# Row 0 by one queue, and a shorter run of idle matmuls ahead of the first product

## The chip, the cores and the metric

The kernel runs on one core of a Trainium2 chip. The metric is the device time of one execution in microseconds (us). TensorE (PE in the profile) multiplies, with its weight loads shown as PEld. VectorE (DVE), ScalarE (ACT) and GpSimd (POOL) work beside it on SBUF and PSUM, and transfers between DRAM and SBUF are issued by SyncE (SP), ACT and POOL and carried by 16 DMA engines.

## The reference, cut to what matters

```python
xn = layernorm(x)                                  # x: 2048 x 640, over the 640
h  = layernorm(xn)
a, b = xn @ dft_hid_re.T, xn @ dft_hid_im.T
fnet  = dft_seq_re @ a - dft_seq_im @ b            # 2048 x 640
mixer = (w2.T @ gelu(w1.T @ h + b1) + b2)          # over the 2048 tokens
out = x + fnet + mixer                             # float32
```

Here the kernel multiplies by the sequence DFT first (the transposed matrix against the normalized rows, both parts real and imaginary) and by the hidden DFT afterwards. The sums are the same.

## The kernel before

All matrix products are made in three passes of float32r operands: every operand is split into a high and a low part by `high` (an ACT copy that rounds) and `low` (a DVE subtraction), and `three` adds high x high, high x low and low x high into one PSUM bank. The `x` rows are cut into 16 blocks of 128 ("row k"), the sequence matrices into pieces of 128 x 512. The sequence product, the hidden product, the up product with the gelu and the down product follow each other. Each step of that list has three parts, `steps[i]`: the high part of a piece, its low part, and the products. `turn_of` runs them with the loads and sums that belong to a step.

The change lies at the very beginning, where the order is written out by hand in `START`, one word for each piece of work:

- The first line gives the loads in SP's order. `x0` is row 0, `b0` the first piece of the sequence matrix (`load`, line 507), `b1` the second, then `x1`, `b2` and so on. `x0` calls `row(0)` (line 545), which loads the first 320 columns of row 0 only. The other 320 columns were already asked of ACT's queue on line 137. That issue waits for a memset of POOL on line 136 that writes 128 of the same columns.
- Row 0 is normalized while it arrives. `M0` takes its moments (line 231, one DVE instruction for each half), `A0` puts them together (line 234), `R0` is the reciprocal root on ACT (line 240, tile `near`).
- `T0-0` and `T0-1` make the high part of piece 0: ACT its first 256 columns (line 151, called from line 196), DVE the other 256 (line 207). Behind ACT's half stands a small idle matmul on that half (line 197).
- `D0-0`, `D0-1`, `D0-3` make blocks of the normalized high part of row 0 on DVE (line 398), `H0-2-4` one on ACT (line 292). Each block is a weight of the first products.
- `P0-0` are the five first products (line 521): weights from row 0, 512 columns of piece 0 moving. Then `P0-1`, `P1-0`, `P1-1`, `P0-2`, `P1-2` follow, 24 products of row 0 altogether, and then `P2` and the rest, which need row 1 (`x1`, moments at line 231 too, high parts by `H1-0-2` and `H1-2-5`).

Ahead of all that stand the idle matmuls of line 148 on a constant: they write a PSUM bank that is used later from the start, and they wait for nothing. There are `WARM` of them, nine of 512 columns and six of 64.

Eight semaphores are handed round among the DMAs of SP and ACT, so SP's ninth and later DMAs each wait for the landing of the one eight places before.

Of the kernel before, what the change touches and what calls it, by code (L numbers as in the profile page):

```python
# [14 lines left out]
P = 128  # L15
S = 2048
D = 640
# [8 lines left out]
CH = 512  # L26
NC = S // CH
H2 = D // 2
EPS = 1e-5
AHEAD = 2  # L30
LOADS = 4
WARM = 15

BLOCK = 10
APART = 2
# [42 lines left out]
def fnet_plus_mixer(  # L78
# [30 lines left out]
    nc = tc.nc  # L109
# [19 lines left out]
    x_rows = [x[t * P : (t + 1) * P, :] for t in range(NS)]  # L129
# [3 lines left out]
        keep.tile([P, 7, D], F32, name="x0", tag="slab4"), keep.tile([P, 1, D], F32, name="x1", tag="slab5"),  # L133
    ]
    x_in = [x_slab[k // 7][:, k % 7, :] for k in range(8)]
    nc.gpsimd.memset(x_in[0][:, H2 : H2 + P], 0.0)
    nc.scalar.dma_start(x_in[0][:, H2:], x_rows[0][:, H2:])
    part_up = [dram.tile([P, 2, D], F32, name=f"up{r}") for r in range(NF2)]
    y_part = [[dram.tile([P, ND, CH], F32, name=f"y{m}{c}") for c in range(NC)] for m in range(2)]

# [3 lines left out]
    psum = [acc.tile([P, CH], F32, name=f"psum{i}") for i in range(8)]  # L144
    idle = nc.const_aps.tensor(1.0, [P, CH], dtype=BF16)
    for i in range(WARM):
        n = CH if i < WARM - 6 else P // 2
        nc.tensor.matmul(psum[7][:, :n], idle[:, :P], idle[:, :n], start=True, stop=True)  # L148

    def high(hi, src):  # L150
# [32 lines left out]
    def cut_piece(source, n, tail=False, stacked=False):  # L183

        held = {}

        def of_tail():
            hi, src = (t.rearrange("p (q c) -> p q c", c=P) for t in (held["piece"][:, 0, :n], source()))  # L190
            return hi[:, :, :TAIL], hi[:, :, P - TAIL :], src[:, :, :TAIL]

        def top(part=None):
            if part:
                hi = held["piece"][:, 0, : n // 2]
                high(hi, source()[:, : n // 2])
                nc.tensor.matmul(psum[7][:, : P // 2], hi[:, :P], hi[:, : P // 2], start=True, stop=True)  # L197
                return
            cut_turn[0] = (cut_turn[0] + 1) % (AHEAD + 1)
            held["piece"] = keep.tile([P, 2, D], R32, name="piece", tag=f"cut{cut_turn[0]}")  # L200
            if tail:
                hi, _, src = of_tail()
                high(hi, src)
            elif part is None:
                high(held["piece"][:, 0, :n], source())
            else:
                nc.vector.tensor_copy(held["piece"][:, 0, n // 2 : n], source()[:, n // 2 :])

        def bottom():
            if tail:  # L210
                hi, lo, src = of_tail()
                low(lo, src, hi)
                return held["piece"][:, 0, :n], None
            hi, lo = (held["piece"][:, i, :n] for i in range(2))
            if stacked:
                last = slice(n - P, n)
                low(hi[TAIL:, last], source()[TAIL:, last], hi[TAIL:, last])
            whole = n - P if stacked else n
            low(lo[:, :whole], source()[:, :whole], hi[:, :whole])
            return hi, lo  # L220

        return top, bottom
# [13 lines left out]
    def root(var, q=None):  # L236

        if q is None:
            q = small.tile([P, NS], F32, name="q")[:, : var.shape[-1]]
        nc.scalar.activation(q, var, AF.Abs_reciprocal_sqrt, bias=eps)  # L240
        return var, q
# [25 lines left out]
    def offset(to, ks):  # L267
        nc.vector.scalar_tensor_tensor(to[:, 1, ks], mv[:, ks, 0], -1.0, to[:, 0, ks], op0=ALU.mult, op1=ALU.mult)
# [134 lines left out]
    def channels(k, j):  # L403

        a = fixed[0][k % 4]
        i = (0, 0, 6, 6)[j] if k < 4 and j < 4 else (1, 1, 2, 2)[j] if j < 4 else None
        if i is None:
            return fifth(a, 0, k // 4), fifth(a, 1, k // 4)
        at = at_slot[i] + j % 2 * P
        return a[:, 0, at : at + P], a[:, 1, at : at + P]  # L410
# [76 lines left out]
    def c_tile():  # L487

        i = c_turn[0] = (c_turn[0] + 1) % 6
        return c_place[i // 3][:, i % 3, :]  # L490

    def store_y(add, m, c, j, t):
        if not add:
            nc.gpsimd.dma_start(y_part[m][c][:, j, :], t)
        else:
            nc.gpsimd.dma_start(y_part[m][c][:, j, :], t, accum_op=ALU.add)  # L496

    def first_columns():


        raw = pieces[1].rearrange("p a q c -> p (a q) c")
        banks = {}
        vq = {}

        def load(i):
            m, k = FIRST[i][:2]
            nc.sync.dma_start(raw[:, FIRST_AT[i], :], dft_seq[m * NC, k])

        def products(w, m, k, j0, j1, passes=(0, 1, 2)):


            late_begin = 4
            js = (range(3), range(3, 5)) if (m, k) == (1, late_begin) else (range(j0, j1),)
            if (m, k) == (0, 0):
                js = ((0, 1, 4, 2, 3),)
            for n, j in ((n, j) for part in js for n in passes for j in part):
                rows, cols = ((0, 0), (0, 1), (1, 0))[n]
                begin, end = (late_begin, 1) if m == 1 and j >= 3 else (0, 5)
                if n == 0 and k == begin:
                    banks[m, j] = psum[(5 * m + j) % 8]  # L520
                nc.tensor.matmul(  # L521
                    banks[m, j], channels(k, j)[rows], w[cols], start=n == 0 and k == begin,
                    stop=n == 2 and k == end, skip_group_check=True,
                )

        def read(m, js):
            for j in js:
                c = c_tile()
                nc.scalar.activation(c, banks[m, j], AF.Copy)
                store_y(False, m, 0, j, c)  # L530

        for i, (m, k, j0, j1) in enumerate(FIRST):
            steps.append(
                cut_piece(lambda i=i: raw[:, FIRST_AT[i], :], CH)
                + (lambda w, *passes, at=(m, k, j0, j1): products(w, *at, *passes),)
            )
        reads[6].append(lambda: read(0, range(ND)))

        extras[11].append(lambda: read(1, range(2)))
        extras[12].append(lambda: read(1, range(2, 4)))  # L540
        extras[13].append(lambda: read(1, range(4, ND)))

        def row(k):
            if k == 0:
                nc.sync.dma_start(x_in[0][:, :H2], x_rows[0][:, :H2])
            else:
                nc.sync.dma_start(x_in[k], x_rows[k])

        def begin_loads(i):
            for f in loads.pop(i):  # L550
                f()

        def top(i, *part):
            steps[i][0](*part)

        def bottom(i):
            ready[i] = steps[i][1]()

        def run(i, *passes):
            steps[i][2](ready[i], passes or (0, 1, 2))  # L560
            if not passes or 2 in passes:
                del ready[i]

        def rooted(k, to=None, by=1):
            ks = slice(k, (to or k) + 1, by)
            vq[k] = root(mv[:, ks, 1], near[:, 0, ks])

        def inverted(k, to=None, by=1):
            inverse(norm[:, 0, slice(k, (to or k) + 1, by)], *vq[k])

        def factored(k, to=None, by=1):
            inverted(k, to, by)
            offset(norm, slice(k, (to or k) + 1, by))

        def whole_row(k, by_vector=False):
            if not by_vector and k not in LAST_ROWS:
                return normalize(k, x_in[k], norm)

            nc.vector.tensor_scalar(
                x_in[k], x_in[k], mv[:, k, 0:1], norm[:, 0, k : k + 1], op0=ALU.subtract, op1=ALU.mult  # L580
            )

        return {
            "x": row, "b": load, "q": begin_loads, "T": top, "B": bottom, "P": run,
            "M": lambda k, *halves: statistics(k, x_in[k], *halves), "A": aggregate,
            "R": rooted, "F": factored, "O": lambda k: offset(near, slice(k, k + 1)), "E": half_beside, "V": factors_beside, "v": lambda k: factors_beside(k, False), "n": lambda k: whole_row(k, True), "e": lambda k: half_beside(k, nc.vector), "w": lambda k: factors_beside(k, False, nc.vector),
            "D": first_hi,
            "m": lambda k: nc.vector.tensor_scalar(less, mv[:, k, 0:1], -1.0, None, op0=ALU.mult),
            "c": lambda k: nc.scalar.activation(near[:, 1, k : k + 1], less, AF.Copy, scale=near[:, 0, k : k + 1]),
            "H": lambda k, *ends: first_rows(k, 0, *ends), "N": whole_row,  # L590
            "L": lambda k, *ends: first_rows(k, 1, *ends),
            "W": lambda k: nc.scalar.activation(one, eps, AF.Abs_reciprocal_sqrt),
        }
# [718 lines left out]
```

## Time and profile before

| | us |
|---|---|
| median of 3 runs | 866.1 |
| lowest, highest | 866.06, 866.36 |
| the profiled execution | 866.67 |
| its span, first to last instruction | 864.8 |
| PE busy | 860.9 |
| PEld busy | 790.1 |
| DVE busy | 695.0 |
| ACT busy | 524.0 |
| POOL busy | 159.9 |

The profiled execution took 1.9 us more than its span, which lies around the first and last instruction. All stretches below are counted from the start of the span. A matmul's shown duration holds the time in which its results drain, and matmuls overlap, so the distance between two starts tells how fast they are carried out. The row of the granted clock shows full speed in every slice.

### The profile page before, as it was taken

Reading aid. Unit: us, or ns where it says so; the run is one execution under the profiler, and the core shown is the slowest. Engines: PE = TensorE matmul, PEld = TensorE weight load, DVE = VectorE, ACT = ScalarE, POOL = GpSimd, SP = SyncE. Lnnn points to the kernel's source line nnn. Section 1 sums busy time; section 2 is a strip of 40 time slices with the busy share of each in tenths; the row PEclk is TensorE's granted clock in tenths of the full one; section 3 lists DMA queues with packets and bytes.
Section 4 is the critical chain, followed back from the end, with each engine's and each line's share of the span. In section 5 each row is a group of like instructions: output and inputs, shape, how many; then the busy total and the mean of one; then the engine's idle time right before and its main releaser. Section 6 shows DMA issues by size and latency. Waiting matters only on the chain.

```text
span 864.8 us, 13911 instructions
## 1 busy us (share of the span) xinstructions
PE 860.9 (100%) x4900; PEld 790.1 (91%) x4900; DVE 695.0 (80%) x1176; ACT 524.0 (61%) x970; POOL 159.9 (18%) x216
## 2 busy tenths in 40 slices
PE   9999999999999999999999999999999999999998
PEld 7888888888888888889999999999999999999998
DVE  7898868758767888677877788888679978987887
ACT  5765576763555555547565556676667866555654
POOL 2222131210020211122110101111322221101211
PEclk9999999999999999999999999999999999999999
DMA  9949586695382746869576666665688798766776
GB/s 339 366 102 271 183 254 226 161 292 152 98 188 31 193 105 131 217 108 200 125 167 160 156 142 195 189 175 160 143 185 182 167 235 224 182 142 126 158 168 149
DMA packets 90293, 154.44 MB, mean 179 GB/s; under 512 B 9008, under 2 KB 37424, under 8 KB 89968
## 3 DMA queue, kind: packets, MB, share of 16 engines
q0 software_dynamic: 25008, 57.52, 35.7%
q1 hardware_dynamic: 64928, 95.80, 33.5%
q8 instruction: 38, 0.62, 0.3%
q14 instruction: 31, 0.25, 0.1%
q10 hardware_dynamic: 288, 0.25, 0.1%
HBM read 99.96 MB, written 58.82 MB: 184 GB/s over the span
## 4 chain that ended last, share of the span: by engine, by line
PE 100%; DVE 0%; DVEq 0%; issue 0%
PE psum L162 32%; PE psum L163 32%; PE psum L165 31%; PE psum L521 3%; PE psum L148 0%; DVE pair L962 0%; PE psum L197 0%; DVEq L1308 0%
## 5 line engine op out<-in xcount | busy, mean ns | idle before, releaser
L154 DVE TENSOR_TENSOR piece<-pieces,piece 128x512 fp32r<-128x512 f32 (+4 forms) x496 | 326.8, 659 | 129.7 <-ACT piece L151 124.1
L151 ACT ACTIVATE piece<-pieces 128x512 fp32r<-128x512 f32 (+3 forms) x472 | 295.4, 626 | 221.8 <-PE psum L165 140.3
L162 PE MATMUL psum<-piece,n 128*128 128x512 f32 x540 | 210.1, 389 | 0.0
L163 PE MATMUL psum<-piece,n 128*128 128x512 f32 x540 | 210.1, 389 | 0.0
L165 PE MATMUL psum<-piece,n 128*128 128x512 f32 x540 | 210.1, 389 | 0.0
L163 PE MATMUL psum<-sdown,piece 128*128 128x320 f32 x392 | 120.8, 309 | 0.0
L162 PE MATMUL psum<-sup,piece 128*128 128x320 f32 x392 | 120.8, 309 | 0.0
L162 PE MATMUL psum<-sdown,piece 128*128 128x320 f32 x392 | 120.8, 309 | 0.0
L163 PE MATMUL psum<-sup,piece 128*128 128x320 f32 x392 | 120.8, 309 | 0.0
L165 PEld LDWEIGHTS psum<-piece,n 128*128 128x128 f32 x540 | 101.4, 188 | 21.1
L162 PEld LDWEIGHTS psum<-piece,n 128*128 128x128 f32 x540 | 101.3, 188 | 21.1
L163 PEld LDWEIGHTS psum<-piece,n 128*128 128x128 f32 x540 | 101.3, 188 | 20.9
L157 DVE TENSOR_TENSOR pieces<-pieces 128x512 f32<-128x512 f32 (+3 forms) x142 | 111.7, 792 | 3.0
L165 PE MATMUL psum<-sup,piece 128*128 128x320 f32 x368 | 113.7, 309 | 0.0
L165 PE MATMUL psum<-sdown,piece 128*128 128x320 f32 x368 | 113.7, 309 | 0.0
L496 POOL DMA_DIRECT2D y<-c x65 | 56.1, 900 | 255.1 <-DVE c L699 153.9
L165 PE MATMUL psum<-shid,piece 128*128 128x320 f32 x280 | 86.5, 309 | 0.0
L163 PE MATMUL psum<-shid,piece 128*128 128x320 f32 x280 | 86.5, 309 | 0.0
L162 PE MATMUL psum<-shid,piece 128*128 128x320 f32 x280 | 86.5, 309 | 0.0
L163 PEld LDWEIGHTS psum<-sup,piece 128*128 128x128 f32 x392 | 73.6, 188 | 0.0
L163 PEld LDWEIGHTS psum<-sdown,piece 128*128 128x128 f32 x392 | 73.6, 188 | 0.0
L162 PEld LDWEIGHTS psum<-sdown,piece 128*128 128x128 f32 x392 | 73.6, 188 | 0.0
(139 smaller groups left out, 1109.5 us busy)
## 6 DMA issues: line engine op xcount, KB each, us to landing
pieces<-in_dft_seq SPq DMA_DIRECT2D x120, 256.0 KB, 5.3
y<-c POOLq DMA_DIRECT2D x105, 256.0 KB, 4.7
pieces<-in_w SPq DMA_DIRECT2D x88, 256.0 KB, 3.9
out<-pair POOLq DMA_DIRECT2D x36, 320.0 KB, 5.7
pieces<-y SPq DMA_DIRECT2D x32, 320.0 KB, 4.0
pieces<-in_w SPq DMA_DIRECT2D x32, 192.0 KB, 2.5
out<-in_x SPq DMA_DIRECT2D x16, 320.0 KB, 7.9
up<-pair POOLq DMA_DIRECT2D x8, 640.0 KB, 3.2
```

The source lines that it names most:

```text
L151: nc.scalar.activation(hi, src, AF.Copy)
L154: nc.vector.tensor_sub(lo, src, hi.bitcast(F32))
L157: nc.vector.tensor_sub(to, a, b)
L162: nc.tensor.matmul(psum, wh, mh, start=first, stop=False, skip_group_check=True)
L163: nc.tensor.matmul(psum, wh, ml, start=False, stop=last and wl is None, skip_group_check=True)
L165: nc.tensor.matmul(psum, wl, mh, start=False, stop=last, skip_group_check=True)
L496: nc.gpsimd.dma_start(y_part[m][c][:, j, :], t, accum_op=ALU.add)
L521: nc.tensor.matmul(banks[m, j], channels(k, j)[rows], w[cols], start=n == 0 and k == begin, stop=n == 2 and k == end, skip_group_check=True,)
```

## The change

Both halves of row 0 are loaded by SP, one behind the other, ahead of all pieces. The memset on POOL and the load on ACT's queue are gone. `WARM` is 16: eight idle matmuls of 512 columns and eight of 64.

```diff
-WARM = 15
+WARM = 16
...
-    nc.gpsimd.memset(x_in[0][:, H2 : H2 + P], 0.0)
-    nc.scalar.dma_start(x_in[0][:, H2:], x_rows[0][:, H2:])
...
     for i in range(WARM):
-        n = CH if i < WARM - 6 else P // 2
+        n = CH if i < WARM - 8 else P // 2
         nc.tensor.matmul(psum[7][:, :n], idle[:, :P], idle[:, :n], start=True, stop=True)
...
             if k == 0:
-                nc.sync.dma_start(x_in[0][:, :H2], x_rows[0][:, :H2])
+                for cols in (slice(0, H2), slice(H2, D)):
+                    nc.sync.dma_start(x_in[0][:, cols], x_rows[0][:, cols])
```

SP's queue at the start of the program, before (`x_76` is the tile of rows 0 to 6, `pieces_125` holds the pieces of the sequence matrix):

```order
L545 DMA x_76<-in_x 128x320
L507 DMA pieces_125<-in_dft_seq 128x512 x2
L547 DMA x_76<-in_x 128x640
L507 DMA pieces_125<-in_dft_seq 128x512
L547 DMA x_76<-in_x 128x640
```

SP's queue at the same place in the changed kernel, whose lines stand one or two lower (`pieces_124` is the same tile there):

```order
L544 DMA x_76<-in_x 128x320 x2
L505 DMA pieces_124<-in_dft_seq 128x512 x2
L546 DMA x_76<-in_x 128x640
L505 DMA pieces_124<-in_dft_seq 128x512
L546 DMA x_76<-in_x 128x640
```

One more DMA of 128x320 stands ahead of the first piece, and all that follow have moved back by one place.

ACT at the start of the program, before:

```order
L137 DMA x_76<-in_x 128x320
L592 ACT_TABLE_LOAD
L592 ACTIVATE one<-eps 128x1
L240 ACTIVATE near<-mv,eps 128x1
L151 ACTIVATE piece<-pieces_125 128x256
```

ACT at the same place in the changed kernel:

```order
L591 ACT_TABLE_LOAD
L591 ACTIVATE one<-eps 128x1
L238 ACTIVATE near<-mv,eps 128x1
L149 ACTIVATE piece<-pieces_124 128x256
L588 ACTIVATE near<-less,near 128x1
```

The DMA is gone and nothing else has moved. On POOL the memset is gone, on DVE the order is as before (the second moments no longer wait for POOL), and on PE the run of idle matmuls switches to 64 columns one place earlier and is one longer. Behind these places the engines' orders are the same as before.

## Rows read from the trace of the kernel before

**Rows 1.** The page: busy us (share) of each engine; a group's busy us, mean ns.

```profile
PE 860.9 (100%) x4900; PEld 790.1 (91%) x4900; DVE 695.0 (80%) x1176; ACT 524.0 (61%) x970; POOL 159.9 (18%) x216
...
L162 PE MATMUL psum<-piece,n 128*128 128x512 f32 x540 | 210.1, 389 | 0.0
```

**Rows 2.** Timeline of PEld: start us, us, instruction, count, idle before.

```profile
1.17 0.15 PEld L148 LDWEIGHTS <-const-bfloat16-1.0 128*128 128x128 bf16 x1 [0.27 <-issue]
...
4.16 0.15 PEld L148 LDWEIGHTS <-const-bfloat16-1.0 128*128 128x128 bf16 x1 [0.28 <-issue]
4.58 0.36 PEld L148 LDWEIGHTS <-const-bfloat16-1.0 128*128 128x128 bf16 x5 [0.28 <-issue]
4.96 0.29 PEld L197 LDWEIGHTS psum<-piece 128*128 128x128 f32 x1
```

**Rows 3.** Timeline of PE in narrow windows, up to 11.6 us.

```profile
0.79 4.32 PE L148 MATMUL psum<-const-bfloat16-1.0 128*128 128x512 bf16 x15 [0.79 <-PEq L1301]
...
5.20 0.78 PE L521 MATMUL psum<-piece,n 128*128 128x512 f32 x1
...
5.77 0.63 PE L521 MATMUL psum<-piece,n 128*128 128x512 f32 x1
...
6.20 0.63 PE L521 MATMUL psum<-piece,n 128*128 128x512 f32 x1
...
7.13 4.47 PE L521 MATMUL psum<-piece,n 128*128 128x512 f32 x19
```

**Rows 4.** Timeline of the other engines and the queues, 0 to 12 us.

```profile
0.75 0.39 SPq L545 DMA_DIRECT2D x<-in_x  x1
...
0.98 0.38 ACTq L137 DMA_DIRECT2D x<-in_x  x1
...
1.20 0.90 SPq L507 DMA_DIRECT2D pieces<-in_dft_seq  x2
...
3.08 0.95 DVE L231 BATCH_NORM_STATS2 st<-x 128x6 f32<-128x320 f32 x2 [3.08 <-DMA x<-in_x]
...
4.31 0.29 ACT L240 ACTIVATE near<-mv,eps 128x1 f32<-128x1 f32 x1 [1.41 <-DVE mv L234]
...
4.51 0.40 ACT L151 ACTIVATE piece<-pieces 128x256 fp32r<-128x256 f32 x1
...
4.64 0.86 DVE L398 TENSOR_SCALAR n<-x,mv,near 128x128 fp32r<-128x128 f32 x3
...
6.54 0.63 ACT L151 ACTIVATE piece<-pieces 128x512 fp32r<-128x512 f32 x1 [0.81 <-DMA pieces<-in_dft_seq]
...
8.55 0.88 DVE L231 BATCH_NORM_STATS2 st<-x 128x6 f32<-128x320 f32 x2
...
10.23 1.20 ACT L292 ACTIVATE n<-x,near 128x256 fp32r<-128x256 f32 x2 [0.23 <-DVE near L268]
```

**Rows 5.** From issue to landing: row 0's half on line 545, then on 137.

```profile
DMA to landing us min/median/max: 2.3/2.3/2.3
...
DMA to landing us min/median/max: 2.5/2.5/2.5
```

**Rows 6.** The same for piece 0, then piece 1, both on line 507.

```profile
DMA to landing us min/median/max: 3.2/3.2/3.2
...
DMA to landing us min/median/max: 4.9/4.9/4.9
```

**Rows 7.** Queues (packets, MB, share) in 1.5:2.4, 2.4:2.9 and 2.9:3.6; q10 is ACT's.

```profile
q1 hardware_dynamic: 93, 0.12, 50.7%
...
q10 hardware_dynamic: 109, 0.14, 77.2%
q1 hardware_dynamic: 53, 0.05, 29.9%
...
q1 hardware_dynamic: 112, 0.23, 93.9%
q10 hardware_dynamic: 35, 0.03, 11.8%
```

## The prediction

> **What bounds the kernel now.** I read the page's busy times first: PE is busy 860.9 of the 864.8 us [rows 1]. So nothing that the change does behind the first product can help, unless it makes PE wait. What is left is the time before PE's real work, and the pace at which its first products run. So I read the first 12 us engine by engine.
>
> On PE, the idle matmuls of 512 columns start 0.427 us apart (seven steps from 1.17 to 4.16), those of 64 columns about 0.053 us (five loads in 0.36 us, the last of them 0.15 long), and the last of the run is done near 4.92. The small matmul on piece 0 follows at 4.96 [rows 2]. The first product starts at 5.20, and the next ones stand 0.43 us apart from 5.77 on; the 19 from 7.13 on stand 0.227 us apart (4.47 us, less the 0.39 that one is shown to take, over 18 steps) [rows 1, 3]. The row of the granted clock shows full speed throughout, so the level is read from the distances: 512 columns in 0.427 us is the level of 1.2 GHz, and 0.227 is near what 2.4 GHz allows. PE worked without a pause from 0.79 on [rows 3], and the level rose between 6.2 and 7.1.
>
> What PE waits for at 4.96 is a chain. Row 0's first half lands and DVE takes its moments at 3.08; the second half's follow 0.46 later (0.95 for both, 0.49 for one). ACT's root is at 4.31, its half of piece 0 at 4.51 for 0.40, and PE's small matmul comes 0.05 behind its end, 4.91 [rows 2, 4]. DVE's blocks of row 0 start at 4.64 for lack of the root, and the first takes about 0.35, so they are ready when the small matmul is through. The idle matmuls end just as this chain does; they don't hold it up.
>
> **The change part by part.**
>
> *Idle matmuls.* One of 512 columns less, two of 64 more: -0.427 + 2 x 0.053 = -0.32 us. The run ends at 4.60 rather than 4.92. PE isn't what decides 4.96, so this gives 0 unless the chain ends sooner, and then 0.32 at most. It opens a pause of some 0.36 us ahead of the small matmul that wasn't there.
>
> *The second half of row 0.* ACT issued it at 0.98; SP will at its second place, 1.20 [rows 4]. Its landing now: 0.98 + 2.5 = 3.48, against 0.75 + 2.3 = 3.05 for the first half [rows 5]. Its moments run 0.06 later than DVE's own pace (later, two such instructions in a row take 0.88 us with 0.48 for one, 0.40 apart [rows 4]), so this landing is on the chain. Slower end: if a landing follows its issue, 1.20 + 2.5 = 3.70, +0.21. Faster end: -0.06, when DVE's pace decides. I take 0, by the nearest rows: until 2.4 only the first half moves, between 2.4 and 2.9 ACT's half has 77% of the engines and both queues together are over 100% [rows 7]. So it starts when the first half leaves the engines, about 2.4, and that is 1.2 us after SP's new issue.
>
> *Piece 0.* SP issues it at its third place, where piece 1 stood: 1.20 + some 0.46 = 1.66 (two issues in 0.90 [rows 4]). Now it lands at 1.20 + 3.2 = 4.40 [rows 6]. If the landing follows the issue it comes 0.46 later, at 4.86; ACT's half of piece 0, which had 0.11 to spare (4.51 - 4.40), then starts 0.35 later, and so does the first product. If the engines decide, 0. Its packets go from 2.9 to 3.6 with the engines full [rows 7], behind the same bytes in either kernel, so I take 0.
>
> *ACT's issue and POOL's memset.* 0.38 us of ACT's queue and one small memset go. ACT sits idle for 1.41 us ahead of its root at 4.31 [rows 4], and POOL isn't on the chain. The activation table is loaded sooner, into that idle time: 0. Without that cover the same would be a gain of 0.38, which nothing shows.
>
> *What is moved back.* Every later DMA on SP goes out one place, some 0.46 us, later until the eight semaphores pace SP by landings, as they do already from about 6.5 on. The nearest thing that waits is piece 1 (landing 1.66 + 4.9 = 6.5, and ACT waits 0.81 us for it [rows 4, 6]); behind its low part DVE takes row 1's moments at 8.55, and ACT's blocks of row 1 follow from 10.23 to 11.43 [rows 4]. PE starts product 25, the first on row 1, one step behind the 24th: 7.13 + 19 x 0.227 = 11.45, and the 27th, the first on the last of these blocks, at 11.90. That leaves 0.47 us. Even +0.46 for piece 1 is just hidden; the cost is 0, and if the cover is gone, what exceeds 0.47.
>
> *Sum.* 0 + 0 + 0 + 0 + 0 against the profiled execution's own 866.67 (span 864.8 and 1.9 around it). That execution lies 0.57 above the median of the runs, so I put the same 0 on the median: 866.1. The unknown costs go from -0.32 to +0.35.
>
> The trace has three products at the slow distance behind the first one, at 0.20 us each (0.427 - 0.227): 0.6 us. The Trainium skill, "TensorE: Matmul & The Clock Gate", Part 1 on the clock gate, says that the moment of the rise isn't tied to the start of the kernel, and that the same kernel shows another number of slow matmuls from run to run. By the row the head of this kernel has a fixed price; by the rule, runs of one kernel differ by such steps, and an estimate of the sum is 866.67 - 0.6 where the rise comes before the products. One trace can't tell them apart; that the shown runs lie 0.3 to 0.6 below the profiled one fits the rule.
>
> **The rivals.**
>
> *The pause costs the clock (slower).* Before, PE worked without a pause from 0.79 until the level rose; now it stands still for about 0.36 us at 4.60. If the rise is counted anew from the end of that pause, it comes 4.96 - 0.79 = 4.17 us later. In 4.17 us the slow level makes 4.17 / 0.427 = 9.8 products, which take 2.22 us at 0.227: +1.95, so 868.05. It decides as soon as a pause this long counts as idle at all. For it: the rise came some 5.4 to 6.3 us after PE's first matmul with no pause between. Against it: the pause is short beside that, and a part of the delay would cost only a part of the 1.95.
>
> *The loads come late.* Landings follow SP's issues after all: +0.35 by piece 0, the larger of the two, so 866.45. For it: piece 1 took 4.9 us from its issue, and the rows can't say how much of that was a queue. Against it: the full engines until 3.6.
>
> *The loads come early.* One queue instead of two: -0.06 if only the second half gains, down to -0.32 if the first half and piece 0 do too and the run of idle matmuls is the next limit; 865.8 to 866.0. For it: a share of 29.9% on q1 beside ACT's half between 2.4 and 2.9, and 11.8% of ACT's beside piece 0 after it. Against: most of the former is the end of the first half. The Trainium skill, "DMA: Bandwidth & Descriptors", Queues, rings and completion order, says that each engine turns between the queues that have work for it, a packet at a time. By that rule piece 0 and the second half took turns before, and one queue would bring the half in first. The shares show an overlap of that kind, but a small one.
>
> The change may also not do what it says, if the chain, not the queue, keeps all times as they are; that is the forecast itself.
>
> **How the numbers follow.** Forecast (no term counts, 866.1): 0.68. Loads late (866.45): 0.12. Loads early (865.9): 0.10. The pause costs the clock (up to 868.05): 0.10. About 0.2% or 1.7 us is what a measurement of this kernel can tell from no change. Only the last rival reaches it, in full and not in part: slower 0.07. Nothing above gives 1.7 us less: faster 0.01. Same 0.92. The range: 866.06 - 0.32 less a little for the runs' spread, 865.6; above, 866.36 + 0.35 and the beginning of the clock's case, 867.0. What it leaves out is most of that case and a few in a hundred beside.
>
> **What would show it.** Forecast: row 0's two landings near 3.05 and 3.5, the root near 4.31, the small matmul near 4.96 behind a pause of PE from 4.60, the first product near 5.20, products 0.43 apart until about 7 and 0.227 from then on. Loads late: ACT's half of piece 0 starts behind 4.7. Loads early: second moments 0.40 behind the first, and the small matmul before 4.9. The clock's case: more than ten products at 0.43. I am wrong if PE waits anywhere behind its first product, above all near 11.9 for row 1, or if the time moves by more than 1 us with the level rising where it did.

## The result and the profile after

| us | before | after |
|---|---|---|
| median of 13 runs | 866.36 | 868.43 |
| lowest, highest | 865.90, 866.67 | 867.07, 869.86 |
| profiled execution | 866.67 | 867.42 |
| its span | 864.8 | 865.7 |

The ratio is 1.0022, 95% from 1.0014 to 1.0030: slower by some 2 us, where no change was forecast. The 13 runs of the changed kernel fall into two groups, six from 867.07 to 867.54 and seven from 868.43 to 869.86. The profiled execution belongs to the lower one, so its trace shows only the first part of the loss. The rest is shown by the experiments.

The page of the changed kernel, busy us of PE and of a group of products, as in [rows 1], and its chain of waits by share:

```profile
PE 860.1 (99%) x4901; PEld 789.5 (91%) x4901; DVE 695.1 (80%) x1176; ACT 523.6 (60%) x970; POOL 158.6 (18%) x215
...
PE psum L160 32%; PE psum L161 32%; PE psum L163 31%; PE psum L519 3%; DMA pieces<-in_dft_seq 0%; SPq L544 0%; ACT piece L149 0%; DVE pair L961 0%; PE psum L195 0%; DVEq L1307 0%
...
L160 PE MATMUL psum<-piece,n 128*128 128x512 f32 x540 | 210.1, 389 | 0.0
```

A product costs what it did. New in the chain is a link of DMA, SP's line 544 and ACT's line 149: the span now goes back to SP's issue of row 0 instead of the idle matmuls.

The weight loads of the changed kernel, answering to [rows 2] (start us, us, instruction, count, idle before):

```profile
4.16 0.47 PEld L146 LDWEIGHTS <-const-bfloat16-1.0 128*128 128x128 bf16 x7 [0.28 <-issue]
6.01 0.19 PEld L195 LDWEIGHTS psum<-piece 128*128 128x128 f32 x1 [1.39 <-ACT piece L149]
6.15 5.86 PEld L519 LDWEIGHTS psum<-piece,n 128*128 128x128 f32 x26
```

The matmuls, answering to [rows 3]:

```profile
0.79 4.00 PE L146 MATMUL psum<-const-bfloat16-1.0 128*128 128x512 bf16 x16 [0.79 <-PEq L1300]
...
6.02 0.30 PE L195 MATMUL psum<-piece 128*128 128x64 f32 x1 [1.23 <-ACT piece L149]
6.16 14.22 PE L519 MATMUL psum<-piece,n 128*128 128x512 f32 x61
```

The idle matmuls end near 4.6 as forecast, but the small matmul starts at 6.02 instead of 4.96: a pause of 1.4 us, not 0.36. (PE's row shows 1.23 of it, since the last idle matmul's shown time reaches past 4.6; from here on pauses are those of PE's rows.) The first product is at 6.16 (before 5.20). Its 61 starts are 0.231 apart ((14.22 - 0.39) / 60), so in this execution the products run at the level of 2.4 GHz from the start. The idle matmuls ahead of the pause stood 0.427 apart, 1.2 GHz: the level rose within the pause.

The other engines and queues, answering to [rows 4]:

```profile
0.75 0.87 SPq L544 DMA_DIRECT2D x<-in_x  x2
1.66 0.43 SPq L505 DMA_DIRECT2D pieces<-in_dft_seq  x1
...
3.10 0.90 DVE L229 BATCH_NORM_STATS2 st<-x 128x6 f32<-128x320 f32 x2 [3.10 <-DMA x<-in_x]
...
4.27 0.29 ACT L238 ACTIVATE near<-mv,eps 128x1 f32<-128x1 f32 x1 [2.03 <-DVE mv L232]
5.55 0.42 ACT L149 ACTIVATE piece<-pieces 128x256 fp32r<-128x256 f32 x1 [0.98 <-DMA pieces<-in_dft_seq]
...
5.55 0.29 DVE L205 CAST piece<-pieces 128x256 fp32r<-128x256 f32 x1 [1.13 <-DMA pieces<-in_dft_seq]
...
8.14 0.63 ACT L149 ACTIVATE piece<-pieces 128x512 fp32r<-128x512 f32 x1 [0.83 <-DMA pieces<-in_dft_seq]
...
8.99 0.88 DVE L229 BATCH_NORM_STATS2 st<-x 128x6 f32<-128x320 f32 x2
...
10.67 1.20 ACT L290 ACTIVATE n<-x,near 128x256 fp32r<-128x256 f32 x2 [0.23 <-DVE near L266]
```

Row 0 is on time: moments 0.41 apart, root 0.04 sooner. Both engines wait for piece 0. Before, ACT's half of it stood at 4.51 with no wait in front. Row 1's blocks come 0.44 later (10.67 against 10.23), but PE needs them later too and doesn't wait.

From issue to landing, row 0's first half and piece 0, answering to [rows 5, 6], and the bytes that the only queue moved in 2.9:3.6, answering to the third part of [rows 7]:

```profile
DMA to landing us min/median/max: 2.3/2.3/2.3
...
DMA to landing us min/median/max: 3.9/3.9/3.9
...
q1 hardware_dynamic: 97, 0.14, 120.0%
```

Piece 0 was issued at 1.66 and landed at 5.53; before it was issued at 1.20 and landed at 4.36. The 16 engines report apart: before, all between 3.90 and 4.36; after, fourteen between 3.96 and 4.79, the last two at 5.51 and 5.53. In 2.9:3.6 the share is over 100% with 0.14 MB, where before 93.9% and 11.8% went with 0.26 MB. So a full share doesn't say that bytes flow: single 2 KB packets of piece 0 last 0.4 to 0.9 us here, where most take 0.1, and that counts as busy.

The last PE rows, of before and then of after:

```profile
861.38 0.31 PE L163 MATMUL psum<-sdown,piece 128*128 128x320 f32 x1
```

```profile
861.76 0.31 PE L161 MATMUL psum<-sdown,piece 128*128 128x320 f32 x1
```

PE's last product starts 0.38 later, but the span ends 0.83 later (864.82 and 865.65): from that product to the end it is 3.45 us before and 3.89 after. The last output lands 2.55 behind PE's last product before and 2.58 after, so 0.41 of the 0.44 lies behind the landing, in what the program does to close.

*The sum for the profiled execution.* First product +0.96; from it to the last product 855.61 instead of 856.18, -0.57, of which some 0.6 are the three slow products of before; the end +0.44; around the span -0.08. Together +0.75, the difference between 867.42 and 866.67.

### The profile page after: what moved, and what is told of

Its sections match the earlier page's. It is cut to its first block, busy times and chain, and to the rows that moved or that the text cites. A ratio compares the mean times of both kernels' runs of the same rounds, so it can differ in the third digit from the quotient of the medians.

```text
span 865.7 us, 13911 instructions
## 1 busy us (share of the span) xinstructions
PE 860.1 (99%) x4901; PEld 789.5 (91%) x4901; DVE 695.1 (80%) x1176; ACT 523.6 (60%) x970; POOL 158.6 (18%) x215
## 4 chain that ended last, share of the span: by engine, by line
PE 99%; DMA 0%; SPq 0%; ACT 0%; DVE 0%; issue 0%; DVEq 0%
PE psum L160 32%; PE psum L161 32%; PE psum L163 31%; PE psum L519 3%; DMA pieces<-in_dft_seq 0%; SPq L544 0%; ACT piece L149 0%; DVE pair L961 0%; PE psum L195 0%; DVEq L1307 0%
```

## The experiments

All times are us. Before is run beside each, with medians of 866.25 to 866.38.

**One half of the change at a time.** *e1* has the loads of the change and the idle matmuls of before:

```diff
-    nc.gpsimd.memset(x_in[0][:, H2 : H2 + P], 0.0)
-    nc.scalar.dma_start(x_in[0][:, H2:], x_rows[0][:, H2:])
...
-                nc.sync.dma_start(x_in[0][:, :H2], x_rows[0][:, :H2])
+                for cols in (slice(0, H2), slice(H2, D)):
+                    nc.sync.dma_start(x_in[0][:, cols], x_rows[0][:, cols])
```

> Both halves of row 0 on SP without the memset, as in the changed kernel, but the fifteen idle matmuls of before (nine of 512, six of 64). Theory A (piece 0, third on SP's queue, lands late; the idle matmuls matter little): piece 0 lands near 5.5, the small matmul comes near 6.0, time about 867.0 to 869.5 with the wide spread of the changed kernel. Rival B (the shorter run of idle matmuls and its pause cost the time): the small matmul near 4.96 to 5.0, time 866.1 to 866.6.

*e2* has the idle matmuls of the change and the loads of before:

```diff
-WARM = 15
+WARM = 16
...
-        n = CH if i < WARM - 6 else P // 2
+        n = CH if i < WARM - 8 else P // 2
```

> The loads and the memset as before, only the idle matmuls changed to eight of 512 and eight of 64. Theory A: piece 0 lands near 4.4, the small matmul stays near 4.96 behind a pause of 0.36 us, time 866.1 to 866.7 with the spread of before. Rival B: that pause alone costs the level, 867 to 868.5 and a wide spread.

e1: 867.87, ratio 1.0023 (1.0014 to 1.0032), runs from 866.51 to 869.99. e2: 866.45, 1.0004 (0.9996 to 1.0013). The new loads alone give the loss within its interval, and the new idle matmuls alone give none that can be told. ACT's half of piece 0 in e1's trace, and the weight loads behind it:

```profile
5.03 0.42 ACT L149 ACTIVATE piece<-pieces 128x256 fp32r<-128x256 f32 x1 [0.45 <-DMA pieces<-in_dft_seq]
...
5.50 0.19 PEld L195 LDWEIGHTS psum<-piece 128*128 128x128 f32 x1 [0.88 <-ACT piece L149]
5.63 6.53 PEld L519 LDWEIGHTS psum<-piece,n 128*128 128x128 f32 x29
```

Here piece 0 landed at 5.01, 0.65 later than before. In e2 the shorter run of idle matmuls leaves a pause of 0.30 (0.49 counted as in the prediction, from 4.60 to the small matmul at 5.09), and two of its 11 runs (868.08 and 868.20) were about 2 above its lowest.

**The place in the queue, and bridging the pause.** *e3* is the changed kernel with row 0 as one DMA of 640 columns, so piece 0 is second again and issued at 1.20:

```diff
-                for cols in (slice(0, H2), slice(H2, D)):
+                for cols in (slice(0, D),):
```

> The changed kernel with row 0 as one DMA of 640 columns on SP, so that piece 0 is the second DMA of SP's queue with the same bytes ahead of it. Theory A with the place in the queue as the cause: piece 0 lands near 4.4; the moments of row 0 start near 3.5 instead of 3.1, the root near 4.7, the small matmul near 5.3 to 5.4, time about 866.3 to 867. Rival C (the bytes, or the moment, not the place): piece 0 lands near 5.5 and the small matmul comes near 6.0 as in the changed kernel, 867 to 869.5.

*e4* is the changed kernel with eleven idle matmuls of 512, which last until 5.7 in its trace:

```diff
-WARM = 16
+WARM = 19
```

> The changed kernel with nineteen idle matmuls, eleven of 512 and eight of 64, so that PE works on until about 5.9. If the spread of the changed kernel (867.1 to 869.9) is the level falling or rising late because of the pause of PE of 1.4 us: the times stay together within 0.6 us, near 867.1 to 867.6. If the spread comes from landings that differ from run to run: the spread stays as wide.

e3: 866.8, 1.0012 (1.0003 to 1.0020). Piece 0 lands at 4.22, as before the change; the whole row lands at 3.51, the small matmul is at 5.35, and five of 11 runs are at 867.96 to 868.56. e4: 867.41, 1.0012 (1.0003 to 1.0021), with all 11 runs between 866.69 and 867.73, a spread of 1.0 where 0.6 was expected. Its PE:

```profile
6.01 0.30 PE L195 MATMUL psum<-piece 128*128 128x64 f32 x1 [0.15 <-ACT piece L149]
6.15 1.25 PE L519 MATMUL psum<-piece,n 128*128 128x512 f32 x4
```

The first product is where it was in the changed kernel, and still the upper group is gone. So the late landing with the longer end costs 1.15 (867.41 against 866.26 beside it), and PE's pause the other 0.9 of the 2.07 that the changed kernel's median lost against its own before. The two medians were not taken side by side, so this split is rough.

**The pause alone.** *e7* is the kernel before with six idle matmuls of 512 and eight of 64; loads and landings stay:

```diff
-WARM = 15
+WARM = 14
...
-        n = CH if i < WARM - 6 else P // 2
+        n = CH if i < WARM - 8 else P // 2
```

> The kernel before with only the run of idle matmuls cut to six of 512 and eight of 64: it ends near 3.75 and PE pauses some 1.2 us ahead of the small matmul, as long as in the changed kernel, but piece 0 lands as before. If the pause by itself moves the rise of the level: the small matmul at 4.96, the times spread from 866.1 to about 868.9 with a median near 867.2, as the changed kernel's do above a floor 1 us higher. If the pause is harmless and the spread of the changed kernel is of its landings: 866.1 to 866.8.

867.9, above the 867.2 expected, 1.0014 (1.0005 to 1.0023): three runs at 866.17 to 866.23, as before, and eight at 867.63 to 868.60. The profiled one is of the latter (868.27). Its matmuls:

```profile
5.10 0.42 PE L197 MATMUL psum<-piece 128*128 128x64 f32 x1 [1.16 <-ACT piece L151]
...
5.33 4.62 PE L521 MATMUL psum<-piece,n 128*128 128x512 f32 x10
...
9.75 4.62 PE L521 MATMUL psum<-piece,n 128*128 128x512 f32 x19
```

The first product is 0.14 later than before. From 5.33 to 9.75 ten products take 0.44 each (0.57 for the first, 0.427 for the others), which is the level of 1.2 GHz; the next ones stand (4.62 - 0.39) / 18 = 0.235 apart. The level that had risen by 7.1 without a pause [rows 3] rises near 10.0. From the first product to the last it takes 857.68 instead of 856.18; that +1.50 and the 0.14 of the first product are the difference between the two profiled executions (868.27 and 866.67, 1.60). The median lost 1.65.

**Rise, fall and rise again, or one late rise?** Four more traces of the changed kernel as it is, for its upper group: *e11*, *e12*, *e14* and *e15*.

> The changed kernel once more, for its trace: in 6 of its 13 runs the mean granted clock was 0.998, in those of 869.3 to 869.9 us above all. Theory E (the level had risen before PE's pause and falls again behind it): in such a run the products start at 0.23 us or are slow from the first on, stand 0.43 apart for some 3.4 us, and the clock's record holds a slow stretch behind a fast one. Rival: in all runs the level only rises late, once.

> The same again, for the same question; a run at 867.1 shows the level at its higher step when the first product starts, a run at 869.5 shows some twelve products 0.43 apart.

> The changed kernel. In a run of 869.3 to 869.9, theory F: some twelve products 0.43 apart, the rise near 11 to 12, no fast one before. Theory E: a fast stretch ahead of the slow one.

> The same question as the run before it: by theory F the time above 867.1 is 0.2 us for each product that stands 0.43 behind the one before it, ten to thirteen of them in a run above 869.2.

They took 868.82, 868.57, 869.15 and 868.90. In e11, e12 and e15 the products stand 0.43 apart until 9.2, 9.1 and 9.3, and the level rises once. In e14 it is otherwise. Its matmuls, and then its stretches by engine, where PEclk, the third number from a row's end, is the granted clock:

```profile
0.79 3.51 PE L146 MATMUL psum<-const-bfloat16-1.0 128*128 128x512 bf16 x16 [0.79 <-PEq L1300]
...
6.18 0.30 PE L195 MATMUL psum<-piece 128*128 128x64 f32 x1 [1.88 <-ACT piece L149]
...
6.92 3.57 PE L519 MATMUL psum<-piece,n 128*128 128x512 f32 x8
```

```profile
core 0: us, PE busy (x) PEld busy (x) DVE busy (x) ACT busy (x) POOL busy (x), PEclk, DMA share, GB/s
0.00:6.00 6.00, 3.51 (x16) 1.43 (x16) 1.57 (x6) 2.07 (x4) 1.36 (x9) 1.00 0.66 181
6.00:8.00 2.00, 1.82 (x6) 1.57 (x7) 2.00 (x7) 1.54 (x4) 0.00 (x0) 0.75 0.92 297
8.00:9.00 1.00, 1.00 (x3) 0.71 (x3) 1.00 (x2) 0.35 (x1) 0.00 (x0) 0.50 1.01 378
9.00:10.00 1.00, 1.00 (x4) 0.80 (x3) 1.00 (x3) 0.28 (x1) 0.00 (x0) 0.50 1.05 403
10.00:11.00 1.00, 1.00 (x5) 0.82 (x4) 0.74 (x5) 0.46 (x2) 0.00 (x0) 0.79 1.06 415
11.00:12.00 1.00, 1.00 (x6) 0.79 (x6) 0.98 (x3) 1.00 (x2) 0.00 (x0) 1.00 1.03 407
```

The whole run of idle matmuls ends at 4.30, 0.3 sooner, since the level rose at 3.6 already. PE stands still for 1.88, the first products start 0.34 and 0.26 apart, and then the granted clock is at half from 7.0 to 10.4. The column shows 1.00 in the first stretch too, where the idle matmuls start 0.427 apart: ahead of the first rise the level has to be read from distances. So the pause can cost in both ways: it delays the first rise, or it takes back one that had come. *e13* makes the pause longer, with piece 0 as SP's fifth DMA behind the loads of the change (idle matmuls of before):

```diff
-    x0 W0 b0 b1 x1 b2 x4 b3 x5 b4 x2 x3 b5 x6 x7 b6 b7
+    x0 W0 b1 x1 b0 b2 x4 b3 x5 b4 x2 x3 b5 x6 x7 b6 b7
```

> The changed kernel's loads with piece 0 only fifth on SP (behind piece 1 and row 1) and fifteen idle matmuls: it lands near 7, and PE pauses some 2 us or more from 4.92 on. Theory F (a pause only puts off the one rise): products 0.43 apart until 10 to 12, then 0.227, or, where the level rose before the pause, 0.23 from the first product on. Theory E (the level falls in the pause): idle matmuls at 0.21 us before the pause and products at 0.43 behind it.

870.33, against 866.38 beside it. Its pause, and the granted clock behind it:

```profile
7.44 0.30 PE L195 MATMUL psum<-piece 128*128 128x64 f32 x1 [2.65 <-ACT piece L149]
```

```profile
8.00:9.00 1.00, 1.00 (x4) 0.81 (x4) 1.00 (x3) 1.00 (x3) 0.00 (x0) 0.50 0.97 356
9.00:10.00 1.00, 1.00 (x4) 0.80 (x3) 1.00 (x3) 0.24 (x1) 0.00 (x0) 0.50 1.02 393
10.00:11.00 1.00, 1.00 (x4) 0.79 (x3) 1.00 (x3) 0.00 (x0) 0.00 (x0) 0.50 1.04 407
11.00:12.00 1.00, 1.00 (x5) 0.77 (x4) 0.76 (x5) 0.30 (x1) 0.00 (x0) 0.95 1.05 413
```

The level had risen at 4.3, during the idle matmuls, and fell behind the pause: the clock is at half until 11.1.

How often each case comes can be read from the mean granted clock on record with every run. Of the 17 traces only e13 and e14, where the level rose, fell and rose again, have 0.998; the others, with one rise, have 0.999 or 1.000. Of the changed kernel's 13 runs five have 0.998 (not six, as e11's expectation says), all of them from 868.91 to 869.86, and in e1 it is the four slowest of 11. So most of the upper group seems to have lost a level that had come. In e7 no run has it: there the loss is one late rise.

The Trainium skill, "TensorE: Matmul & The Clock Gate", Part 1, says that one kernel shows another number of slow matmuls from run to run. The two groups of runs agree with that, and show what goes with it: in 13 runs with PE at work from the start to the products (before) the spread was 0.8, with the pause 2.8. Of all 93 recorded runs of before, none took more than 867.03.

**What sets piece 0's landing: its place or the moment of its issue?** *e5* puts row 0's halves on SP and piece 0 on ACT's queue (issued at 1.34):

```diff
-    x0 W0 b0 b1 x1 b2 x4 b3 x5 b4 x2 x3 b5 x6 x7 b6 b7
+    x0 b0 W0 b1 x1 b2 x4 b3 x5 b4 x2 x3 b5 x6 x7 b6 b7
...
-            nc.sync.dma_start(raw[:, FIRST_AT[i], :], dft_seq[m * NC, k])
+            if i == 0:
+                nc.gpsimd.memset(raw[:, FIRST_AT[0], :], 0.0)
+            (nc.sync if i else nc.scalar).dma_start(raw[:, FIRST_AT[i], :], dft_seq[m * NC, k])
```

> Both halves of row 0 on SP as in the changed kernel, but piece 0 issued by ACT, the first DMA of ACT's queue, held back by a POOL memset to about 1.4 us; fifteen idle matmuls as before. Piece 0 is now nobody's third DMA, with the same bytes ahead of it. Theory A (the third place on SP's queue is what lands late): piece 0 lands at 4.2 to 4.6, the third of SP (piece 1) lands late instead, after 5; the small matmul comes near 5.0, time 866.1 to 866.8. Rival C (what moves behind the two halves lands late, whichever queue): piece 0 lands after 5, 867 and more.

866.73, 1.0005 (0.9996 to 1.0014). A miss: the small matmul is at 5.55. Piece 0 lands at 5.06 (15 engines by 4.53), and the half of row 0 beside it at 4.10 instead of 3.48, with both queues moving bytes at once. *e6* is before without its memset, so that ACT issues at 0.75:

```diff
-    nc.gpsimd.memset(x_in[0][:, H2 : H2 + P], 0.0)
```

> The kernel before with only the memset left out, so that ACT issues the second half of row 0 at about 0.75 instead of 0.98, beside SP's first half. Theory A: piece 0 stays second on SP's queue and lands near 4.4; the two halves take turns on the engines, so the first moments may start up to 0.4 later (3.1 to 3.5) and the second right behind; time 866.0 to 866.8. A rival in which the memset is what the changed kernel misses: 867 and more.

866.44, 1.0003 (0.9994 to 1.0012). Now both halves are issued at 0.75, move at the same time and land at 3.64 and 3.80; the first one's moments start at 3.66. The memset of before kept the second half behind the first. *e8* keeps piece 0 second and delays its issue by a memset on POOL that it must wait for (to 1.48), *e9* by a larger one (to 1.66, the moment of the change):

```diff
+            if i == 0:
+                nc.gpsimd.memset(raw[:, FIRST_AT[0], :], 0.0)
             nc.sync.dma_start(raw[:, FIRST_AT[i], :], dft_seq[m * NC, k])
```

> The kernel before, with a POOL memset of piece 0's tile ahead of its load, so that SP issues piece 0 at about 1.6 as in the changed kernel, but still as the second DMA of its queue. If the place in the queue is what counts: piece 0 lands at 4.2 to 4.6 and the time is 866.1 to 866.8. If the moment of issue is what counts: it lands after 5, as in the changed kernel, and the time is 867 and more.

> The kernel before, with a POOL memset of 736 columns in the pieces' tile ahead of the first load, so that SP issues piece 0 near 1.65 as the changed kernel does, still second on its queue and with the second half of row 0 on ACT. Theory D (the landing follows the issue, most engines some 2.7 us behind it and the last ones later): most of piece 0 by 4.4 to 4.5, the last near 5.0 to 5.5, time 866.9 to 868. Theory A in the form of the place in the queue: all of it by 4.4 to 4.6, time 866.2 to 866.8.

In e9 the memset's columns are `raw[:, 0:2, :368]`. *e10* instead puts a tiny load ahead of piece 0, which is third then and issued at 1.66:

```diff
+                nc.sync.dma_start(keep.tile([P, 4], F32, name="tiny"), x_rows[15][:, :4])
```

> The kernel before with one tiny load (128 x 4 columns, read by nothing) between row 0's first half and piece 0 on SP, so that piece 0 is third on SP's queue and is issued near 1.65, with the same bytes ahead of it as before. Theory D: as in the run with the late issue, the last of piece 0 near 5.0 to 5.5, time 866.9 to 868. If neither issue nor place counts but the half of row 0 ahead of it on the same queue: piece 0 lands near 4.4 and the time is 866.2 to 866.8.

e8: 866.63, 1.0005 (0.9996 to 1.0015), piece 0 at 4.99, between the expectations. In e6 one of ten runs (868.41) and in e8 two (867.95 and 868.56) are of an upper group as well; the highest of each is the profiled one. There PE pauses 0.37, and the products stand 0.43 apart until 9.7 and 9.3. e9: 867.59, 1.0016 (1.0007 to 1.0026), piece 0 at 5.43 although it is second. Its rows:

```profile
1.66 0.34 SPq L509 DMA_DIRECT2D pieces<-in_dft_seq  x1
...
5.52 0.42 ACT L151 ACTIVATE piece<-pieces 128x256 fp32r<-128x256 f32 x1 [0.76 <-DMA pieces<-in_dft_seq]
...
5.99 0.30 PE L197 MATMUL psum<-piece 128*128 128x64 f32 x1 [0.88 <-ACT piece L151]
```

So third place isn't needed for a late landing; the later issue, with the loads behind it put off too, is enough. In e10 piece 0 lands at 6.18, later than either expectation. Its time, 879.03 (1.0149, 1.0132 to 1.0166), says nothing on this: its products take longer throughout (below).

| piece 0 issued | landed, in the order of the names |
|---|---|
| 1.20 (before, e2, e3, e6, e7) | 4.36, 4.21, 4.22, 4.39, 4.53 |
| 1.34 (e5), 1.48 (e8) | 5.06, 4.99 |
| 1.66 (e1, e4, e9, after) | 5.01, 5.52, 5.43, 5.53 |
| 1.66 (e11, e12, e14, e15) | 5.30, 5.21, 5.69, 5.45 |

The middle one of the 16 engines reports 2.5 to 3.0 us behind the issue in all of them. What grows is the spread: 0.2 to 0.5 us from the first engine to the last behind an issue at 1.20, 0.8 to 1.7 behind a later one (2.1 in e10), mostly by the last one to four engines. Why these lag stays open, and with it why the cost is more than the delay of the issue.

None of these kernels beats the one before.

## Why the prediction was wrong

*Idle matmuls: right alone, wrong beside the loads.* The run ended at 4.6, and e2's interval holds no change, though two of its 11 runs were some 2 slower. But the term was sized with a pause of 0.36, and beside the loads it became one of 1.4.

*The second half of row 0: right.* Landing forecast at 3.48, found at 3.475. ACT's issue and the memset: 0, as forecast. What moved back: no wait at row 1, as forecast.

*Piece 0: the step that failed.* "Its packets go from 2.9 to 3.6 with the engines full [rows 7], behind the same bytes in either kernel, so I take 0." The landing came 1.17 later and the first product 0.96. I read the share as bytes, and the engines as the limit. The runs show the landing moving by 0.65 to 1.33 for an issue 0.46 later (the table, and e9, where the order and the queue of every load stayed). The upper end of +0.35 was too low as well: it took the landing to follow the issue one for one, and left out the last engines. Even so piece 1, issued at 1.66 in the kernel before, took 4.9 [rows 6] and was the nearest row for a DMA at that place. It was named for the rival and not used as the bound; by it the late end of piece 0's landing is 1.66 + 4.9 = 6.56, and 5.53 lies inside.

*The pause costs the clock: the rival that came.* Its size was about right: up to +1.95 forecast, +1.65 in e7's median, some 0.9 between e4 and the changed kernel. In e7 its mechanism fits too, a late rise with ten slow products, seven more than in before's trace, where 9.8 more were forecast. In most of the changed kernel's upper runs it was another: the level had risen and was lost again (e14, and the mean clocks of 0.998). That the rival's 868.05 lies near the measured 868.43 is luck, as it had the landing on time and the end unchanged. Its chance was too small in part because the pause was taken to be 0.36, but e2, e6 and e8 have slow runs too, with pauses of 0.30 and 0.37 in their traces. It doesn't come in every run: in the one trace of the lower group the level rose inside the pause, and the pause cost nothing.

*The end of the program: a term that was missing.* From PE's last product to the end it takes 3.45 before and 3.89 to 3.91 in all five traces of after. It is the same 3.88 to 3.90 in e1, e4 and e13, which have one DMA more on SP than before, and 3.44 to 3.48 in e2, e5, e6, e7, e8 and e9, which have as many as before. e3, with as many too, has 3.56, and e10, with one more but longer products, 4.35. That it goes with the count, e3 and e10 apart, is all that is shown; what SP does there wasn't tested.

For the median of 868.43, 2.07 above before, this makes +1.15 by e4 (late landing and end, less what an early rise gives back) and some +0.9 by the pause.

## What to carry to other kernels

Where the first load that PE needs is moved back one place, take as the bound of its landing the DMA that stood at that place before, down to the last of its engines, and don't read a full share of the engines as full use. A run of idle matmuls must reach up to the first product: a pause between them cost 0 to 2.8 us here, and differently from run to run; bridged (e4), none of 11 runs lost it. Before a wait is closed or opened at the head of a kernel, ask both what it delays and what it does to PE's level.

## What the hardware showed that I had not expected

- Single packets of 2 KB took 0.35 to 1.4 us among others of 0.1 in the first 6 us, in the kernel before too. The Trainium skill, "DMA: Bandwidth & Descriptors", Latency and other measured facts, gives 0.2 us for an access of HBM on average and 2 us at high load; the sizes agree, but no run here shows that this is the cause.
- One DMA more on SP went with an end 0.44 us longer, nearly all of it behind the last landing.
- In e10 a tile of 16 bytes for each partition more went with products of 512 columns 0.231 to 0.233 apart rather than 0.227 through the sequence product. Its page shows it in the mean of a group (394 ns instead of 389 [rows 1]):

```profile
L162 PE MATMUL psum<-piece,n 128*128 128x512 f32 x540 | 212.8, 394 | 0.0
```

That is some 10 of its 13 us; whether the places of the other tiles do it wasn't tested.
